# Weights of the gated layers and the output projection: loaded from the ScalarE queue instead of SyncE's, with the written-out order drawn up anew

## The chip, the cores and the metric

The kernel runs on one core of one Trainium2 chip. The metric is the device time of one execution in microseconds, as the median of several runs. The engines are called as in the profile: PE (TensorE, matmul; PEld is its weight load), DVE (VectorE), ACT (ScalarE), POOL (GpSimd) and SP (SyncE). A "q" behind a name (SPq, ACTq) means the sequencer of that engine, which issues DMAs.

## The reference, cut to what matters

Four layers are applied to one sequence x of 2048 rows and 512 columns, each with a layernorm ahead of it and a residual sum behind it: A, B, A, B. A is a linear attention whose features are softmaxes (32 heads of 16), B is a gated feed-forward layer of width 1376. Both A layers use the same weights, and so do both B layers.

```python
def _A_ref(x, wqkv, w_phi, wo):
    qkv = (x @ wqkv) ...                                   # split into q, k, v by head
    pq, pk = einsum(q, w_phi), einsum(k, w_phi)
    phi_q = concat([softmax(pq), softmax(-pq)]); phi_k = the same of pk
    kv = einsum("bhsf,bhsd->bhfd", phi_k, v);  z = sum_s phi_k
    o = einsum(phi_q, kv) / (einsum(phi_q, z) + 1e-6)
    return o @ wo                                          # output projection
def _B_ref(x, W_gate, W_up, W_down):
    gate = x @ W_gate;  up = x @ W_up
    gate = gate * (gate > 0)
    return (gate * up) @ W_down
x = x + _A_ref(layernorm(x), ...); x = x + _B_ref(layernorm(x), ...)   # twice
```

## The kernel before, in words

The sequence is cut into 16 row tiles of 128 rows. x stays in SBUF for the whole execution (`x_sb`), and is added to in place. The work goes by these names, which are the ones the recorded operations carry:

- `A0` and `A2` are the two attention layers, `B1` and `B3` the two gated layers, and `L0` to `L3` the layernorms ahead of them.
- In an attention layer, for every tile t: `k t` and `v t` (projections on PE, lines 725 and 766), `expk t` (ACT), `Zk t` and `rZk t` (sum and reciprocal on DVE), `phik t` (normalising, POOL or DVE), `kvacc t` (PE adds this tile to kv in two PSUM banks). Once all 16 tiles are in, `kvbd` and `kvf` on DVE take kv out of PSUM (`kv_fin`, line 792). Then the queries: `q t` or, for tiles 2 to 9 of A0, `q 2 c` and `q 6 c` for four tiles at once, `expq`, `num t` (PE), a division, `o t`, a transpose `otr t` and the output projection `wo t` (line 942), and `resid`.
- In a gated layer, for up to four tiles at once and for each of 11 slices fc of the width: `Wg` and `Wu` (PE, line 962; `gu` for the last, short slice), `relu` (ACT), on some slices `up` (ACT), `h` (DVE), and then `down t`, 11 matmuls that add all slices of tile t (line 1011), `resid`, and in the last layer `store`.
- Transposes of 128-row tiles (`L0 tr`, `A0 qtr`, `A0 otr`, `B1 htr`, `L1 tr`) are mostly done by DMA and issued by SP; tiles 0 to 3 of L0, and tiles 0 and 1 later on, are transposed on PE (`ytr`, `otr`, `tr`) and copied out by DVE or ACT.
- PE also gets 70 `dummy` matmuls on a tile of ones in the first 20 us, whose results are not used.

**What sets the order.** The kernel first records all operations, 3963 of them, with what each reads and writes. It doesn't order them itself: for each engine the string `ORDER` lists the numbers of its operations, in base 36, in the order in which they are issued, and `CHOICE` names an engine for those small operations that two engines can do (`op2`, line 433). `schedule` (line 229) goes through these lists with assumed durations and gives each operation a start. These assumed durations only decide how waits are numbered; [...]

**The weights that the change is about.** `late_weights` (line 605) records 18 loads from HBM: `wo0` to `wo3` (128 KB each, line 609), `Wg0` to `Wg3` and `Wu0` to `Wu3` (344 KB each, line 612), `Wd0` to `Wd4` (256 KB each, line 614) and `Wdl` (96 KB, line 615), some 4.5 MB together. Each takes as its read the transposed tile `("yT", 15)` of L0 (line 1061), so none can be issued before the transpose `L0 tr 15` has landed. They are first used by `A0 wo 0`, by `B1 gu 0 10` and the `B1 Wg` and `B1 Wu` behind it, and by `B1 down 0`, and stay in SBUF for the second pair of layers. The first loads of the kernel, x and the first attention weights, come earlier: x, `phi` and the transposed query weights `wqT` from SP, `wv` and `wk` from ACT (lines 542 to 555).

In the order before, the 18 loads stand in SP's list between transposes:

```
L0 tr 15, L0 tr 13, L0 tr 12, Wu2, L0 tr 14, Wd0, Wd4, wo1, Wdl, Wg1, A0 qtr 0 1, A0 qtr 0 0, Wd2, wo3,
A0 qtr 1 1, A0 qtr 1 0, Wg2, Wg0, wo0, Wg3, wo2, Wu0, Wd1, Wu1, Wu3, A0 otr 2, Wd3, A0 otr 3, B1 htr 0, ...
```

Of the kernel before, what the change touches and what calls it, by code (L numbers as in the profile page):

```python
# [14 lines left out]
        "29 26 6 25 27 28 2a 2b 4t 2c 39 49 3u 4y 4e 44 5i 5n 58 5s 4j 6j 6k 67 73 72 8l 6d 84 6a 4o 83 8k 91 9x 9y 7r 96 9z c4 c5 9b c6 9g d9 da db b4 f9 f8 "  # L15
        "fm fl ay ee ef b2 eg gz gy fz h0 hx hw fy ij g5 g4 ik gb ga gg gh ii hv mk mj n4 n3 mu mt lm lq lt ne nd nn no nt r8 o5 o4 rf of op oq jv kn p0 pa pb "
        "vg pl pw pv vk q6 qg qh qr s1 ko sd sc sn xw xt sx sy t8 lg tt tj ti zn u4 ue u3 zu up uo uz wd wo wp x9 wz xa m8 ru ym yn xk z7 11o z8 yx 10k 11s zi "
        "10l 11v 10v 142 w2 12t yb 149 146 134 13p 135 13f 109 159 14z 13q 15a 15u 12a 15v 15k 14o 16x 178 177 17i 1b7 16m 18l 1aw 1c9 1db 1ad 1by 1d0 1e6 1dv "
        "1ea 1f0 1fg 1ew 1em 1gj 1fw 1gk 1fc 1gi 1jm 1hk 1hl 1hj 1kb 1fs 1ib 1ic 1kr 1l7 1g8 1ia 1j2 1j3 1gx 1ll 1lk 1j1 1m9 1ma 1nv 1k6 1ob 1mz 1my 1lj 1or "
        "1l3 1kn 1p7 1nn 1m8 1mn 1no 1mx 1pl 1pk 1ly 1q9 1nm 1o7 1nc 1qa 1pj 1qz 1qy 1on 1rq 1rp 1q8 1s4 1p3 1qx 1s3 1py 1ro 1t5 1t6 1s5 1s6 1t8 1qn 1t7 1u7 "  # L20
        "1ua 1u8 1xr 1uw 1uv 1u9 1xx 1y3 1uy 1ym 1yn 1ux 1z1 1z2 1y9 1yl 1zh 1zg 1z0 1zv 1zw 1zf 24t 1zu 24u 255 24v 24w 256 258 230 257 25u 25t 25h 25i 25k "
        "25w 25v 25j 26q 271 27d 272 22j 27n 27c 27z 27o 27y 289 28a 28l 28k 28v 28w 297 29h 296 29i 29t 29s 2be 23c 23x 2bp 2bq 24i 2cc 2cb 2c1 26f 2c0 2dj "
        "2cn 2cm 2di 2dt 2b3 2e5 2du 2e4 2ef 2eg 2er 2eq 2ft 2fu 2hu 2i5 2i6 2ih 2ig 2j2 2ir 2j3 2a7 2is 2d7 2kg 2k6 2kh 2k5 2l2 2l3 2ks 2kr 2mh 2le 2mg 2ld "
        "2fi 2hb 2ju 2m5 2qa 2pz 2qb 2n8 2ql 2qw 2qx 2qm 2sa 2r7 2sl 2sb 2r8 2ny 2sw 2sx 2t7 2sm 2pg 2t8 2um 2tj 2ti 2ul 2g8 2rz 2mv 2ua 2vw 2x5 2ak 2v0 2xg "
        "2xr 2xh 2od 2y3 2xs 2y2 2vd 2yd 2yp 2ye 2yo 2z0 2zb 2yz 2zm 2za 2zl 2gl 2wo 2zw 2zx 308 2wb 307 30z 2oq 31c 30m 322 "),
    "dve": (
        "2z 30 33 3a 3b 3e 3l 3m 3v 3k 3w 3p 2m 53 3z 5d 5x 5z 5t 5v 5u 60 5y 5w 7i 7g 7f 7h 6l 64 6m ao 74 ap 75 an am 85 7t 86 8m a0 7x 8n 7v a3 a1 a4 c7 ca "
        "c8 cb dc df b0 fa dg fn dd fo fb eh ek el ei em h1 h2 fq h4 hy hz h5 i1 il im i0 in io j2 j1 j3 j4 ix jd iz je iy j0 k6 jj k7 ku ky l1 l2 jo l3 l4 jp "
        "l6 l7 lv lw ju kc ly lz nu kh rc rg ki rh og ld ri o6 le or p1 rk pc pm rl vn vo q7 m5 px vq qi m6 xp qs kp s2 vs so se r4 sz xy xz t9 rr tk tu y1 u5 "
        "uf uq zr 13s we lh v0 zw zx zy zz rs vc 13t vz x0 wq w0 y8 y9 xb yo xl 13v 106 107 17w yy 15x zj 15y m9 z9 17x 15z 10m 17y 1b9 1ba 19o 10w 12u 11y 181 "  # L30
        "19p 14c 120 121 136 118 14d 13g 16c 14e 16d 150 19r 1cb 127 11k 13r 15b w3 128 1cc 18b 18c 15w 15l 1cd 14l 14m 16y 16j 16k 17j 179 17v 18i 18j 1a3 1a4 "
        "1bo 1bp 19b 1cq 1cr 18z 1aa 1ab 1b8 1dl 1ax 1dm 19n 1bv 1cx 1bw 1cy 1ca 1e8 1ds 1dt 1e7 1eb 1dc 1ey 1fe 1f3 1fh 1d1 1en 1ex 1jk 1kp 1fu 1fx 1gl 1fj "
        "1ft 12b 1k9 1fd 1l8 1ks 1gy 1dw 1hm 1g9 1hn 1j4 1j5 1gm 1id 1ha 1go 1nt 1l5 1nw 1mb 1ie 1i1 1hp 1mc 1la 1o9 1is 1k7 1jj 1p5 1oc 1gn 1os 1op 1ko 1p8 "
        "1lm 1ln 1n0 1ig 1n1 1n2 1l4 1lo 1pm 1lz 1lp 1nd 1np 1mo 1j7 1nq 1pn 1po 1r0 1pp 1r1 1o8 1r3 1qb 1qc 1s7 1s8 1oo 1p4 1rr 1rs 1se 1sf 1pz 1qo 1t9 1tg "
        "1rf 1xp 1ta 1th 1qe 201 1xs 1sw 1xv 202 203 20f 1xu 1ty 1tl 204 20g 1y1 208 209 1yo 1um 1y7 1y6 1yp 1z3 1ya 1yq 1z4 1yc 1zi 1zj 1zl 1zx 1zy 200 1zz "
        "20a 21r 21q 21s 21p 20d 221 222 227 22u 22v 22c 23n 23o 22d 20m 22i 248 249 235 236 265 23b 20n 2et 26r 266 2gm 2eu 24f 23u 23v 273 2ev 27e 2gn 280 "
        "28b 27p 2at 24g 2au 28m 2go 2lg 298 2cx 29j 28x 29u 2cy 2j5 26c 2j6 26d 2n9 2na 2f8 2f9 2bf 23d 2a6 2lh 2br 2aj 2li 2ll 2b0 2h1 2cd 2c2 2h2 2d4 2ff "
        "2co 23y 2b1 2or 2os 2dk 2nc 2d5 2fg 2e6 2eh 2dv 2es 2tl 2fv 2jk 2jl 2g7 2ra 2ou 2b4 2hv 2rb 2i7 2ow 2lv 2tm 2lw 2gk 2it 2h8 2h9 2ii 2j4 2no 2m2 2k7 "
        "2np 2rf 2m3 2jr 2js 2l4 2ki 2kt 2p6 2p7 2lf 2mi 2mu 2rp 2nv 2nw 2rq 2n7 2m6 2u0 2u1 2qc 2q0 2hc 2jv 2op 2oc 2vm 2pd 2qn 2qy 2pe 2r9 2sc 2rw 2rx 2vn "
        "2t9 2sn 2sy 2tk 2un 2uz 2u7 2u8 2vt 2vu 2vc 2x6 2xt 2ub 2xi 2wa 2yf 2wn 2y4 2yq 2s0 2zn 2z1 2zy 2zc 309 30l 30y 31b 31o 320 "),  # L40
    "pool": (
        "2p 0 1 4 2t 5 2w 2x 31 2 2u 2n 2o 32 3c 34 3d 3n 3o 2y 3x 3y 3f 2s 2r 2q 2v 61 62 66 63 69 6c 3 7j 7l 7k 7m 7n 7o 6n 7p 7q 76 ar aq as au at 87 av aw "
        "ax 8o a2 a5 c9 cc dh fp fc de fd ff ej h3 fs en h6 l5 lu lx rj jw vp jx vr vt xx kq y0 zv y2 100 13u 13x 17z li 11w rv 160 11x 14a 14b ma 162 19q 1bb "
        "1be 11z 10a yc 19t 14f 1bc yd 1cg rw w4 1ce 10b 18m 14p 1ec 16n 1ed 1f1 1f2 1fi 1fy 1fz 1jn 1kc 1kd 1bz 18n 16o 1ke 14q 1jo 1kt 1jp 1c0 1ku 1l9 1ae "
        "1ho 12c 1nx 1p9 1dx 1pa 1if 1od 1md 1ny 1oe 1ot 1j6 1d2 1ou 1me 1n3 1af 1r2 1nr 1ns 1sg 1sj 1s9 1sc 1rt 1qd 1sa 1tb 1te 1tc 1xt 206 1sh 1ti 1tj 20h "
        "1y4 1y5 20k 1xy 1xz 1y0 1ru 1yr 1yb 1z6 1z5 1zk 20i 20b 20o 20r 20p 2ew 2gr 2gp 22k 22l 2ey 2j7 2j8 23e 26g 2ja 24j 2nb 24k 23z 2lj 2ot 2b5 2tn 2to "
        "2tq 2d8 26h 2ne 2rc 2rd 2d9 2hd 2fj 2fk 2nz 2o0 2jw 2vx 2ph 2m7 2s1 2pi 2uc 2vy "),
    "pe": (
        "7 8 9 a b c d e f g h i j k 4p 4q 4r 4s l m n o p q r s t u v w x y z 35 36 37 38 10 11 12 13 14 15 16 17 3g 3h 3i 3j 18 45 46 47 48 3q 3r 3s 3t 4z 50 "
        "51 52 59 5a 5b 5c 4u 4v 4w 4x 4a 4b 4c 4d 40 41 42 43 5e 5f 5g 5h 4f 4g 4h 4i 5j 5k 5l 5m 19 1a 1b 54 55 56 57 1c 1d 1e 5o 5p 5q 5r 1f 1g 6f 6g 6h 6i "  # L50
        "1h 6y 6z 70 71 1i 1j 1k 1l 1m 1n 1o 8g 8h 8i 8j 1p 1q 1r 1s 6p 1t 1u 7z 80 81 82 1v 1w 6o 1x 1y 1z 20 21 22 23 24 4k 4l 4m 4n 9l 9m 9n 9o 8x 8y 8z 90 "
        "9h 9i 9j 9k 9p 9q 9r 9s 9t 9u 9v 9w 6q 6r 6s 6t 77 78 79 7a 92 93 94 95 bo bp bq br bs bt bu bv 6u 6v 6w 6x 97 98 99 9a 88 89 8a 8b bw bx by bz c0 c1 "
        "c2 c3 ct cu cv cw 9c 9d 9e 9f cx cy cz d0 d1 d2 d3 d4 d5 d6 d7 d8 f4 f5 f6 f7 fh fi fj fk 7b 7c 7d 7e 8c 8d 8e 8f 8p 8q 8r 8s dy dz e0 e1 a6 a7 a8 a9 "
        "e6 e7 e8 e9 e2 e3 e4 e5 ea eb ec ed fu fv fw fx ae af ag ah cd ce cf cg cl cm cn co 8t 8u 8v 8w aa ab ac ad gm gn go gp gi gj gk gl ai aj ak al ch ci "
        "cj ck gq gr gs gt gu gv gw gx di dj dk dl g0 g1 g2 g3 hn ho hp hq dq dr ds dt ia ib ic id cp cq cr cs dm dn do dp hr hs ht hu g6 g7 g8 g9 du dv dw dx "
        "es et eu ev eo ep eq er gc gd ge gf ie if ig ih mb mc md me mf mg mh mi f0 f1 f2 f3 ew ex ey ez h7 h8 h9 ha hf hg hh hi i2 i3 i4 i5 ip iq ir is hb hc "
        "hd he hj hk hl hm i6 i7 i8 i9 it iu iv iw j5 j6 j7 j8 j9 ja jb jc mz n0 n1 n2 mv mw mx my k2 k3 k4 k5 jf jg jh ji jy jz k0 k1 ml mm mn mo mp mq mr ms "
        "kr ks kt kv kw kx kz l0 jk jl jm jn lj lk ll ln n5 n6 n7 n8 lo lp lr ls n9 na nb nc nf ng nh ni nj nk nl nm jq jr js jt k8 k9 ka kb r5 r6 r7 r9 np nq "
        "nr ns kd ke kf kg ob oc od oe o0 o1 o2 o3 nw nx ny nz ra rb rd re o7 o8 o9 oa ol om on oo oh oi oj ok l9 la lb lc os ot ou ov kj kk kl km p6 p7 p8 p9 "
        "p2 p3 p4 p5 vd ve vf vh ow ox oy oz m1 m2 m3 m4 pr ps pt pu pd pe pf pg pn po pp pq ph pi pj pk vi vj vl vm py pz q0 q1 q8 q9 qa qb q2 q3 q4 q5 qc qd "  # L60
        "qe qf qj qk ql qm xm xn xo xq rx ry rz s0 qn qo qp qq qt qu qv qw qx qy qz r0 r1 r2 r3 s8 s9 sa sb s4 s5 s6 s7 sf sg sh si xr xs xu xv sj sk sl sm sp "
# [295 lines left out]
ACT = mybir.ActivationFunctionType  # L357
AX = mybir.AxisListType
P = 128
# [17 lines left out]
CHOICE = {}  # L377
# [38 lines left out]
class Kernel:  # L416
# [96 lines left out]
    def setup(self):  # L513
        op, dma, r = self.op, self.dma, self.r
        k = self
# [698 lines left out]
```

The softmax here doesn't subtract the row's maximum and nothing guards it: scores larger than these inputs give would overflow.

## Time and profile before

| | |
|---|---|
| median of 8 runs | 379.36 us (378.92 to 379.82) |
| the profiled execution's own time | 379.82 us |
| its span, first to last instruction | 377.6 us |
| granted TensorE clock | 1.0 throughout |
| moved by DMA | 29.33 MB, of it 25.86 MB on SP's queue (q1) and 3.05 MB on ACT's (q10) |
| HBM read, written | 7.91 MB, 2.10 MB |

The page gives for each engine the time in which it was busy, then the span in 40 slices of 9.44 us with the busy share of each in tenths. A group of instructions carries its line, its tile and its mean duration. DMA issues carry the time that the sequencer took and the time from issue to landing. "A <- B" in an idle time means that A's wait ended with B. The profiled execution is one; its own time is 2.2 us more than its span and lies at the upper end of the runs.

### The profile page before, as it was taken

Reading aid. Unit: us, or ns where it says so; the run is one execution under the profiler, and the core shown is the slowest. Engines: PE = TensorE matmul, PEld = TensorE weight load, DVE = VectorE, ACT = ScalarE, POOL = GpSimd, SP = SyncE. Lnnn points to the kernel's source line nnn. Section 1 sums busy time; section 2 is a strip of 40 time slices with the busy share of each in tenths; the row PEclk is TensorE's granted clock in tenths of the full one; section 3 lists DMA queues with packets and bytes.
Section 4 is the critical chain, followed back from the end, with each engine's and each line's share of the span. In section 5 each row is a group of like instructions: output and inputs, shape, how many; then the busy total and the mean of one; then the engine's idle time right before and its main releaser. Section 6 shows DMA issues by size and latency. Waiting matters only on the chain.

```text
span 377.6 us, 6882 instructions
## 1 busy us (share of the span) xinstructions
PE 368.4 (98%) x2519; PEld 204.6 (54%) x2565; DVE 276.1 (73%) x607; ACT 227.0 (60%) x463; POOL 131.1 (35%) x234
## 2 busy tenths in 40 slices
PE   7999999999999999999999999999999999999997
PEld 5554555877744454454444446577664454445443
DVE  5999998989968666459799999898984654342323
ACT  3999878765744127874676568584635451653450
POOL 6799941132344001350463577023221201000020
PEclk9999999999999999999999999999999999999999
DMA  7632894313424444320300034435443442142012
GB/s 229 177 78 51 193 238 145 75 33 56 78 43 92 97 66 84 70 30 14 69 2 1 2 79 91 85 63 99 79 83 75 81 86 55 28 71 69 30 42 69
DMA packets 87856, 29.33 MB, mean 78 GB/s; under 512 B 79792, under 2 KB 86800, under 8 KB 87824
## 3 DMA queue, kind: packets, MB, share of 16 engines
q1 hardware_dynamic: 84368, 25.86, 33.7%
q10 hardware_dynamic: 3456, 3.05, 2.5%
q8 instruction: 20, 0.33, 0.4%
q14 instruction: 12, 0.10, 0.1%
HBM read 7.91 MB, written 2.10 MB: 27 GB/s over the span
## 4 chain that ended last, share of the span: by engine, by line
PE 84%; POOL 7%; DVE 3%; issue 2%; ACT 1%; DMA 1%; SPq 0%; POOLq 0%; DVEq 0%
PE ps L962 37%; PE ps L1011 20%; PE ps L725 7%; PE ps L942 7%; POOL expk L750 5%; PE ps L822 5%; PE ps L988 3%; PE ps L921 2%; DMA x_sb<-in_A_x_dram 1%; PE ps L787 1%; PE ps L886 1%; DVE Zk L744 1%; POOL rstd L648 1%; PE ps L868 1%; DVE expk L755 0%
## 5 line engine op out<-in xcount | busy, mean ns | idle before, releaser
L962 PE MATMUL ps<-yT,Wgu 128*128 128x512 bf16 (+2 forms) x870 | 150.8, 320 | 0.6
L962 PEld LDWEIGHTS ps<-yT,Wgu 128*128 128x128 bf16 x880 | 78.5, 98 | 58.8 <-ACT expk L970 1.0
L964 ACT ACTIVATE gate_sb<-ps 128x512 bf16<-128x512 f32 (+2 forms) x110 | 50.7, 480 | 55.3 <-PE ps L962 41.2
L1011 PE MATMUL ps<-Wd,hT 128*128 128x512 bf16 (+4 forms) x354 | 79.3, 373 | 0.5
L1011 PEld LDWEIGHTS ps<-Wd,hT 128*128 128x128 bf16 (+1 forms) x363 | 34.7, 98 | 39.5 <-DVE hT L972 0.7
L972 DVE TENSOR_TENSOR hT<-gate_sb,expk 128x512 bf16<-128x512 bf16 (+2 forms) x70 | 23.9, 360 | 30.4 <-ACT expk L970 21.4
L970 ACT ACTIVATE expk<-ps 128x512 bf16<-128x512 f32 (+2 forms) x70 | 32.0, 475 | 22.2 <-PE ps L962 19.5
L710 ACT ACTIVATE sq<-x_sb,nmr 128x512 bf16<-128x512 bf16 x48 | 34.6, 721 | 10.3 <-DVE x_sb L687 6.6
L744 DVE TENSOR_REDUCE Zk<-expk 128x64 f32<-128x1024 bf16 x32 | 38.1, 1203 | 0.9 <-ACT expk L737 0.7
L714 POOL TENSOR_TENSOR rstd<-rv,mone 128x1 f32<-128x1 f32 x32 | 18.7, 589 | 50.2 <-DVE rv L712 50.0
L1013 DVE SCALAR_TENSOR_TENSOR x_sb<-ps,rstd,x_sb 128x512 bf16<-128x512 f32 (+2 forms) x33 | 23.9, 728 | 15.9 <-PE ps L1011 13.2
L942 PE MATMUL ps<-wo_p,oT 128*128 128x512 bf16 x118 | 30.9, 379 | 0.6 <-DVE oT L413 0.3
L975 DVE TENSOR_TENSOR hT<-gate_sb,ps 128x512 bf16<-128x512 bf16 (+2 forms) x40 | 21.7, 544 | 12.6 <-ACT gate_sb L964 6.4
L855 POOL TENSOR_TENSOR expq<-expq,rho 128x256 bf16<-128x256 bf16 x36 | 22.2, 624 | 24.4 <-DVE rho L852 23.6
L847 DVE TENSOR_REDUCE Zq<-expq 128x64 f32<-128x1024 bf16 x24 | 28.8, 1204 | 0.8 <-POOL rho L852 0.5
L687 DVE SCALAR_TENSOR_TENSOR x_sb<-ps,x_sb 128x512 bf16<-128x512 f32 x32 | 21.9, 687 | 8.6 <-PE ps L942 7.8
L750 POOL TENSOR_TENSOR expk<-expk,rZk 128x1024 bf16<-128x1024 bf16 x13 | 25.9, 2005 | 0.6 <-DVE rZk L746 0.6
L755 POOL TENSOR_TENSOR expk<-expk,rZk 128x512 bf16<-128x512 bf16 x17 | 19.1, 1134 | 11.8 <-DVE rZk L746 11.5
L822 PE MATMUL ps<-Wqp,yT 128*128 128x512 bf16 x91 | 22.7, 379 | 0.3
L725 PE MATMUL ps<-Wkp,yT 128*128 128x512 bf16 x84 | 22.0, 379 | 0.2
L725 PE MATMUL ps<-wv_p,yT 128*128 128x512 bf16 x85 | 21.9, 379 | 0.2
L712 POOL TENSOR_SCALAR rv<-rv 128x1 f32<-128x1 f32 x22 | 4.4, 205 | 45.1 <-ACT sq L710 45.1
(126 smaller groups left out, 515.4 us busy)
## 6 DMA issues: line engine op xcount, KB each, us to landing
out_dram<-x_sb ACTq DMA_DIRECT2D x15, 128.0 KB, 1.7
x_sb<-in_A_x_dram SPq DMA_DIRECT2D x3, 512.0 KB, 5.2
Wgu<-in_B_W_up_dram SPq DMA_DIRECT2D x4, 344.0 KB, 6.1
Wgu<-in_B_W_gate_dram SPq DMA_DIRECT2D x4, 344.0 KB, 4.2
Wd<-in_B_W_down_dram SPq DMA_DIRECT2D x5, 256.0 KB, 3.6
yT<-ytile SPq DMA_TRANSPOSE x56, 2.5
qT<-expq SPq DMA_TRANSPOSE x40, 2.5
hT<-in_A_wqkv_dram ACTq DMA_DIRECT2D x4, 128.0 KB, 4.3
```

Source lines behind the costliest of these rows:

```text
L710: op("act", lambda e: e.activation(k.sq[:], k.x_sb[:, t, :], ACT.Square, scale=-float(D), bias=k.nmr[:, t, :], accum_out=k.rv1[:, t, :]), ...
L725: op("pe", (lambda ic, bank, W: lambda e: e.matmul(k.pb[bank][:], k.yT[:, ic, t * 128:(t + 1) * 128], W[:, ic, :], start=(ic == 0), stop=( ...
L744: op("dve", lambda e: e.tensor_reduce(k.Zk[:, zb, :], k.expk[:, t, :, :, :].rearrange("p g s (h f) -> p (g s h) f", f=16), AX.X, ALU.add), ...
L750: op("pool", lambda e: e.tensor_tensor(kv, kv, k.rZk[:, rb, :].unsqueeze(2).to_broadcast([P, 64, 16]), ALU.mult), [r("expk", t, 0), r("exp ...
L822: op("pe", (lambda ic, bank, tt: lambda e: e.matmul(k.pb[bank][:], k.yT[:, ic, tt * 128:(tt + 1) * 128], k.Wqp[:, ic, :], start=(ic == 0), ...
L847: op("dve", lambda e: e.tensor_reduce(k.Zq[:, b, :], k.expq[:, t, :, :, :].rearrange("p g s (h f) -> p (g s h) f", f=16), AX.X, ALU.add), ...
L942: op("pe", (lambda c, bank: lambda e: e.matmul(k.pb[bank][:], k.oT[:, ob, c, :], k.wo_p[:, c, :], start=(c == 0), stop=(c == NC - 1)))(c, ...
L962: op("pe", (lambda bank, W, ic, fc, Mf: lambda e: e.matmul(k.pb[bank][0:Mf, 0:n], W[:, ic, fc * 128:fc * 128 + Mf], k.yT[:, ic, c0:c0 + n] ...
L964: op("act", (lambda Mf, gb, gs: lambda e: e.activation(k.gate_sb[0:Mf, gs, 0:n], k.pb[gb][0:Mf, 0:n], ACT.Relu))(Mf, gb, gs), [self.RP[gb] ...
L970: op("act", (lambda Mf, ub, up: lambda e: e.activation(up[0:Mf, 0:n], k.pb[ub][0:Mf, 0:n], ACT.Copy))(Mf, ub, up), [self.RP[ub]], ru, 170 ...
L972: op("dve", (lambda Mf, up, gs, u: lambda e: e.tensor_tensor(k.hT[0:Mf, u, 0:n], k.gate_sb[0:Mf, gs, 0:n], up[0:Mf, 0:n], ALU.mult))(Mf, u ...
L1011: op("pe", (lambda fc, Kf, u, c0, bank, m0, m1: lambda e: e.matmul(k.pb[bank][:, m0:m1], k.hT[0:Kf, u, c0:c0 + 128], k.Wd[0:Kf, fc, m0:m1] ...
```

## The change

Four things change; the recorded operations, what they compute and what they depend on stay the same 3963.

1. The 18 loads of `late_weights` are recorded for ACT's queue, no longer for SP's.
2. `ORDER` is another order for all five engines, from the first instruction to the last. The loads now stand among ACT's operations (below). SP's list holds transposes and first loads only.
3. `CHOICE` sends 97 small operations from POOL to DVE or back (49 to DVE, 48 to POOL), five copies from DVE to ACT (`L0 ytrcopy 1`, `A0 otr 0 copy`, `A0 numcp 5 2`, `6 0`, `7 1`) and five from ACT to DVE (`A0 numcp 3 1`, `6 2`, `8 1`, `9 0`, `9 2`).
4. An assumed duration (the first activation, with its table load: 1450 became 250) and the way in which `L0 apply` names its second possible engine. No `L0 apply` changes its engine by it.

```diff
 late_weights:
-   ... dma("sp", lambda e: e.dma_start(k.wo_p[:, c, :], self.A_wo[...]), [rd], [r("wo", c)], 131072, f"dma wo{c}")
+   ... dma("act", lambda e: e.dma_start(k.wo_p[:, c, :], self.A_wo[...]), [rd], [r("wo", c)], 131072, f"dma wo{c}")
-   ... dma("sp", lambda e: e.dma_start(W[:, c, :], src[...]), [rd], [r(nm, c)], 128 * F * 2, f"dma {nm}{c}")
+   ... dma("act", lambda e: e.dma_start(W[:, c, :], src[...]), [rd], [r(nm, c)], 128 * F * 2, f"dma {nm}{c}")
-   ... dma("sp", lambda e: e.dma_start(k.Wd[:, 2 * j:2 * j + 2, :], ...), [rd], [r("Wd", j)], 262144, f"dma Wd{j}")
+   ... dma("act", lambda e: e.dma_start(k.Wd[:, 2 * j:2 * j + 2, :], ...), [rd], [r("Wd", j)], 262144, f"dma Wd{j}")
-   ... dma("sp", lambda e: e.dma_start(k.Wd[0:96, 10, :], ...), [rd], [r("Wd", 5)], 96 * 1024, "dma Wdl")
+   ... dma("act", lambda e: e.dma_start(k.Wd[0:96, 10, :], ...), [rd], [r("Wd", 5)], 96 * 1024, "dma Wdl")
 setup:
-   op("act", ... ACT.Exp), [r("ones")], [r("sq"), r("tbl")], 1450, "table")
+   op("act", ... ACT.Exp), [r("ones")], [r("sq"), r("tbl")], 250, "table")
 ln:
-   self.op2("act" if on_act else "dve", apply, dep, dst, {"dve": 407, "act": 825}, f"{tag} apply {t}", 250.0)
+   how = CHOICE.get(f"{tag} apply {t}", "act" if on_act else "dve")
+   other = "act" if how == "dve" else "pool" if t < 9 and how == "act" else "dve" if how == "act" else "act"
+   dd = {"dve": 407, "act": 825, "pool": 2090}
+   self.op2(how, apply, dep, dst, {e: dd[e] for e in (how, other)}, f"{tag} apply {t}", 250.0)
 ORDER, CHOICE: all strings new
```

ACT's new list around the loads, in names:

```
... A0 expk 10 1, A0 expk 10 0, wo0, Wu2, L0 apply 14, A0 vcopy 10, A0 expk 12 0, A0 expk 12 1, Wg1, Wu1,
A0 vcopy 12, A0 expq 2 0 0, Wu0, A0 expk 14 1, wo3, A0 expk 14 0, A0 expq 2 0 1, A0 expq 2 1 0, A0 expk 15 0,
A0 expq 2 1 1, A0 expk 15 1, A0 expq 2 2 0, Wd2, A0 expq 2 2 1, A0 expq 2 3 0, A0 expq 2 3 1, Wg2, A0 vcopy 14,
wo2, A0 vcopy 15, A0 expq 6 0 0, Wg3, A0 expq 6 0 1, wo1, Wu3, Wd4, A0 otr 0 copy, Wg0, A0 expq 10 1, ...
B1 relu 0 10, A0 numcp 4 0, B1 up 0 0, B1 relu 0 0, Wdl, A0 numcp 4 2, B1 relu 0 1, B1 up 0 2, L1 var 0, Wd0,
B1 relu 0 2, L1 tr 1 copy, Wd3, B1 relu 0 3, A0 numcp 5 0, B1 relu 0 5, B1 relu 0 4, Wd1, B1 up 0 4, ...
```

SP's list begins `x0, x3, x1, x2, phi, x4, x8, wqT, x12` (before: `x0, x1, x3, x2, phi, x4, x8, x12, wqT`), ACT's `wk0, table, wv2, wv0, wv1, wv3, wk2, wk1, wk3` (before: `wk0, wv1, table, wv0, wv2, wv3, wk1, wk2, ...`).

## The prediction

> **What bounds the kernel now.** I read the page first (busy shares and slices), then PE's waits, then the busy time by stretches, then the issues of SP and the two other queues around the loads.
>
> ```profile
> PE 368.4 (98%) x2519; PEld 204.6 (54%) x2565; DVE 276.1 (73%) x607; ACT 227.0 (60%) x463; POOL 131.1 (35%) x234
> ...
> PE   7999999999999999999999999999999999999997
> ...
> DVE  5999998989968666459799999898984654342323
> ACT  3999878765744127874676568584635451653450
> ```
>
> PE is busy 368.4 of 377.6 us. At most 9.2 us of idle time, and the dummies, are to be had at all. The waits of PE that the profile names are fewer still:
>
> ```profile
> PE ps L539 <- POOL ones L527: 1.6, 1, 1.6
> PE ps L678 <- DVE ytile L670: 0.9, 1, 0.9
> PE ps L886 <- DVE expk L413: 0.5, 1, 0.5
> PE ps L942 <- DVE oT L413: 0.3, 1, 0.3
> ```
>
> They are 4.2 us in all with four smaller ones; 1.6 is the start of the program. No named wait is on a late weight. The busy time by stretch says where another engine stands behind PE (columns: stretch, length, then PE, PEld, DVE, ACT, POOL busy):
>
> ```profile
> 16.00:53.00 37.00, 36.73 (x296) 19.53 (x299) 36.51 (x52) 35.36 (x54) 33.90 (x37) 1.00 0.58 114
> ...
> 54.00:66.00 12.00, 11.01 (x81) 6.05 (x83) 10.16 (x26) 8.10 (x11) 1.50 (x3) 1.00 0.55 183
> 66.00:75.00 9.00, 8.90 (x119) 7.43 (x120) 8.56 (x27) 7.03 (x23) 1.22 (x4) 1.00 0.33 72
> 75.00:225.00 150.00, 149.15 (x878) 78.23 (x894) 118.84 (x263) 88.37 (x194) 53.81 (x101) 1.00 0.28 51
> ```
>
> From 16 to 53 us four engines are full at once: PE, DVE (36.51 of 37), ACT (35.36), POOL. DVE's chain there sets when kv is complete. After 75 us PE has nothing to gain: 0.85 idle in 150. So a change can help only in the first 66 us, and can hurt anywhere. Around the loads SP looks like this:
>
> ```profile
> 43.24 0.43 SPq L612 DMA_DIRECT2D Wgu<-in_B_W_gate_dram  x1
> 43.71 2.50 SPq L858 DMA_TRANSPOSE qT<-expq  x2
> 46.26 0.58 SPq L614 DMA_DIRECT2D Wd<-in_B_W_down_dram  x1
> ```
>
> One load costs SP 0.43 to 0.58 us, a transpose about 1.25. SP works through the loads from 38.5 to 55.2, and one more at 65.5. And ACT, where they go:
>
> ```profile
> 45.15 1.09 ACT L737 ACTIVATE expk<-ps 128x512 bf16<-128x512 f32 x2 [0.49 <-PE ps L787]
> ...
> 48.51 2.14 ACT L871 ACTIVATE expq<-ps 128x512 bf16<-128x512 f32 x4
> ```
>
> From 45.15 to 51.6 ACT runs back to back; its idle times in 37 to 53 are 0.53, 0.49 and 0.33.
>
> [...] The trace agrees that position in the row matters: most transposes land 2.5 us after issue, the two that transpose qT at 43.71, behind five loads, land 6.1 and 5.3 us after theirs. [...] The trace of before shows what this means for an ACT that issues a DMA, in a store of the last layer:
>
> ```profile
> 290.00 1.09 ACT L964 ACTIVATE gate_sb<-ps 128x512 bf16<-128x512 f32 x2 [2.20 <-PE ps L962]
> 290.78 0.35 ACTq L1023 DMA_DIRECT2D out_dram<-x_sb  x1
> 290.97 1.09 ACT L970 ACTIVATE expk<-ps 128x512 bf16<-128x512 f32 x2
> ```
>
> The next activation starts at 290.97, 0.48 after the one ahead of it (290.49), the pitch it also has with no DMA between. SP was issuing a transpose then, and the store's issue was no longer (0.35).
>
> **The change, part by part.** The sum is made against the profiled execution (span 377.6, own time 379.82).
>
> *SP is freed.* 18 issues, 0.43 to 0.68 each, 9.0 us. Who waited for them? The transposes behind them: `L0 tr 14`, `A0 qtr 0` and `1`. Tile 14 landed at 42.6 and its k runs at 44.1. The q transposes landed at 49.9 to 52.4 and `num 0` runs at 53.66, after kvbd on DVE. All covered by the DVE chain, at least 1.2 us to spare. Gain 0; if that cover were gone it would be 3 us.
>
> *ACT gets 18 issues.* Thirteen stand between 38 and 54 us, each behind activations with a pitch of 0.48 (512 columns) or 0.92 (1024). By the store an issue hides behind one activation. Where two or three stand together (wo0 and Wu2, Wg1 and Wu1, wo1 with Wu3 and Wd4) issue exceeds cover: 1.03 against 0.92, 1.0 against 0.92, 1.5 against 0.92. That is 0.1, 0.1 and 0.6; the last falls before ACT's 2.2 us idle at 54 to 56. ACT's idle 0.53, 0.49, 0.33 swallows the others. Bounds: 0, and 6 x 0.48 = 2.9 us ahead of `expk 15 1` if nothing hides. I take 0. The wait of wo0 on tile 15's transpose is new on ACT, with `L0 apply 14` behind it; that transpose landed at 36.7, and ACT reaches the load at about 38.2. Cost 0, with 1.5 us to spare.
>
> *The loads land where they are used.* wo0 to wo3 before 60 us and Wg, Wu before 65.7: last issued are wo1, Wu3 and Wg0 at 54 to 57.5, landing times of 3.3 to 6.8 are seen, so 61 to 64: fits. Wdl, Wd0, Wd3 and Wd1 are now issued among the relus of `B1`, from 68 on; the latest is Wd1, reckoned under the rivals. I take 0.
>
> *The start.* x1 is now the third SP load, not the second. Second and third landed at 3.99 and 6.11 before, the fourth at 6.87. DVE's lines there:
>
> ```profile
> 5.47 0.35 DVE L666 TENSOR_SCALAR ytile<-x_sb,mv 128x512 bf16<-128x512 bf16 x1
> 6.89 0.69 DVE L623 BATCH_NORM_STATS2 stats<-x_sb 128x6 f32<-128x512 bf16 x1 [1.07 <-DMA x_sb<-in_A_x_dram]
> ...
> 8.30 0.41 DVE L413 COPY yT<-ps 128x512 bf16<-128x512 bf16 x1
> ```
>
> DVE idled 1.07 for x2. Now it idles from 4.6 to about 6.1 for x1, 1.5, and then x2 is there. Against that, the copy at 8.30 (0.41) goes to ACT, which idles then. On DVE: 1.5 - 1.07 - 0.41 = 0.0. On PE `v 1` stands behind the transpose of tile 2, whose `apply 2` moves behind BD (0.69) and comes 0.5 to 0.9 later; `comp wk 0` is now ahead of it; I reckon `v 1` at 10.4 for 10.18. ACT, full from there to the first expk, passes this on: +0.2. Bounds: if x1 lands 0.5 earlier, because ACT's second load now stands behind the table activation and its wait for the ones (about 1.6 instead of 1.24), -0.3; if it doesn't and tile 3 slips too, +0.6.
>
> *Everything else* is the same operations in another order. From 16 to 53 DVE has the same set of work. In 54 to 66 DVE loses the copy of otr 0 (0.36) and gets ab 2, zm 3 and numcp 3 1 (about 1.1) for zd 2 and zd 3 (0.37), while L1 apply 0 moves behind tsc 2: by my count 64.4, and PE asks for it at 64.67. 0. After 75 us I take 0; PE's waits there have no room to gain 0.8.
>
> Sum: 0 + 0 + 0 + 0.2 + 0 = +0.2. Span 377.8, own time 380.0; the median stands 0.46 below that execution, so 379.56, that is **379.6**. A measurement of this kernel can tell about 0.2%, 0.76 us, from no change, so this is no change.
>
> **The rivals.**
> *ACT's issues are not hidden* (slower). 2.9 us ahead of `expk 15 1`; ACT's idle takes 1.0, and from its end (48.68) to Zk 15 (49.48) there are 0.8. DVE's chain, and with it kv, would be 1.1 late, the later issues add up to 0.7: 381.4. It decides from 0.30 us per issue (1.8 over six). Against it: the store above, but that ACT had just idled.
> *Wd1 comes late* (slower). It stands behind relu 0 5 and relu 0 4: before, relu 0 3 and 0 4 ran at 70.71, numcp takes 0.55, two relus about 0.5, so issue at 71.8. These loads took 2.9 (alone) to 3.6 (median) to land: 74.7 to 75.4. `down 0` starts at 74.98 and wants it at its third matmul, 75.4. From 3.6 us on each further tenth is one of PE; at 4.5, +0.9: 380.5.
> *A new stall in the dense part* (slower). The order is new for 300 us in which PE waited for nothing. Some transposes need 4.1 to 4.3 us, not 2.5; an order that has only 0.6 to spare loses 1.1 once: 380.7.
> *Faster.* The copy off DVE counts (0.4), x lands earlier (0.3), and of the 0.5 that PE idles around the second kv, 225 to 250, most goes: -0.9 to -1.1 against my sum, 378.5. For it: DVE's chain of the first layer has next to no gaps. Against it: ACT must follow.
> *The loads hide anyway*, so that the change of queue does nothing and only the order counts, is what my sum says.
>
> **How the numbers follow.** No change 0.37 (its own range 378.7 to 380.3); faster 0.27; ACT not hidden 0.13, Wd1 late 0.12, new stall 0.11, together slower 0.36. The range leaves out the far end of faster (below 378.2, 0.08) and of the slow cases (above 381.4, 0.10): 378.2 to 381.4.
>
> **What would show it.** Right: ACT's pitch of 0.48 and 0.92 stays with loads between; transposes of q land in 2.5 to 4 us; kvbd at 53.0 to 53.4; `down 0` without a wait; PE's idle after 75 us as before. Wrong: idle of ACT with nothing released by another engine at the loads; a wait of line 1011 on a DMA; stats of tile 1 later than 6.3; a PE wait above 0.5 us behind 75 us.

## The result, and the profile after

The kernel after takes **381.35 us** in the median of 12 runs (380.08 to 382.07), the kernel before beside it 379.36 in 32. The ratio is 1.0043 with a 95% interval of 1.0034 to 1.0053: slower by 0.4%, small and certain. The forecast was no change at 379.6; the time lies inside the range (378.2 to 381.4), by 0.05 at its upper edge.

The runs don't lie evenly. Five are between 380.08 and 380.49, seven between 381.24 and 382.07, and none in between; the kernel before has nothing of the kind (378.76 to 380.5; of 94 later runs of it, beside the experiments, one is above that, 381.01). So there are two things to find: what costs every run about 0.9 us, and what costs half of them 1.3 more. The profiled execution of the kernel after took 380.14 and has a span of 378.4 (before: 377.6), so it is one of the lower group. Behind the layernorm's code its lines stand three later than in the kernel before (725 is 728, 766 is 769, 886 is 889, 1011 is 1014).

The page of the kernel after, busy time and slices:

```profile
PE 367.1 (97%) x2520; PEld 203.1 (54%) x2565; DVE 277.6 (73%) x608; ACT 227.1 (60%) x463; POOL 123.5 (33%) x233
...
PE   6999899999999999999999999999999999999997
```

PE has an 8 in its fifth slice (37.8 to 47.3 us). Every slice behind it is as full as before. PE's waits say what the 8 is:

```profile
PE ps L539 <- POOL ones L527: 1.6, 1, 1.6
PE ps L769 <- DMA yT<-ytile: 1.4, 1, 1.4
PE ps L681 <- DVE ytile L669: 1.3, 1, 1.3
```

The second line is new: a k projection waits 1.4 us for a transpose by DMA. The third is the start, where PE now idles for x1 (before, 0.9 for another tile). The busy time by stretches shows where the time is lost and where not (length, then PE, PEld, DVE, ACT, POOL, as in the prediction):

```profile
16.00:53.00 37.00, 35.20 (x252) 18.06 (x256) 35.61 (x51) 34.08 (x52) 33.77 (x37) 1.00 0.57 113
...
75.00:225.00 150.00, 149.10 (x893) 78.52 (x907) 121.00 (x269) 87.04 (x193) 47.34 (x95) 1.00 0.28 51
```

In 16 to 53 us PE, DVE and ACT all lost busy time (36.73 to 35.20, 36.51 to 35.61, 35.36 to 34.08): a gap that stops the three of them. After 75 us PE is as busy as before (149.10 for 149.15). The gap itself, in ACT's part of the timeline (start, length, engine, line, operation):

```profile
36.03 0.34 ACTq L609 DMA_DIRECT2D wo_p<-in_A_wo_dram  x1
36.17 0.85 ACT L662 ACTIVATE ytile<-x_sb,nmr,rstd 128x512 bf16<-128x512 bf16 x1
36.40 0.58 ACTq L612 DMA_DIRECT2D Wgu<-in_B_W_up_dram  x1
36.88 1.98 ACT L772 ACTIVATE expk<-ps 128x1024 bf16<-128x1024 f32 x2
...
42.57 1.02 ACT L772 ACTIVATE expk<-ps 128x1024 bf16<-128x1024 f32 x1 [2.10 <-PE ps L769]
```

`wo0` and `Wu2` stand in ACT's list behind both `expk` of tile 10. Those run at 36.88 to 38.86, but the loads went out at 36.03 and 36.40: 0.85 and 0.48 us before the first of the two activations that stand ahead of them had begun. While they went out ACT still ran `L0 apply 12` (line 662), whose result is what `L0 tr 12` transposes. So the loads overtook the very transpose that the k of tile 12 waits for. `L0 tr 12` follows at 37.05 on SP. The DMA issues of that moment (KB, then time from issue to landing), first of the kernel before, then of the kernel after:

```profile
yT<-ytile SPq DMA_TRANSPOSE x1, 2.4
```

```profile
Wgu<-in_B_W_up_dram ACTq DMA_DIRECT2D x1, 344.0 KB, 4.5
yT<-ytile SPq DMA_TRANSPOSE x1, 4.4
```

The transpose is the same and from the same queue, issued 0.2 earlier than before (37.05 for 37.27). It landed 1.8 later, at 41.45 for 39.69.

### The profile page after: what moved, and what is told of

Its sections match the earlier page's. It is cut to its first block, busy times and chain, and to the rows that moved or that the text cites. A ratio compares the mean times of both kernels' runs of the same rounds, so it can differ in the third digit from the quotient of the medians.

```text
span 378.4 us, 6894 instructions
## 1 busy us (share of the span) xinstructions
PE 367.1 (97%) x2520; PEld 203.1 (54%) x2565; DVE 277.6 (73%) x608; ACT 227.1 (60%) x463; POOL 123.5 (33%) x233
## 4 chain that ended last, share of the span: by engine, by line
PE 91%; DVE 2%; DMA 2%; ACT 2%; issue 1%; SPq 0%; ACTq 0%
PE ps L965 37%; PE ps L1014 20%; PE ps L728 10%; PE ps L945 7%; PE ps L825 5%; PE ps L769 3%; PE ps L991 3%; PE ps L790 2%; PE ps L871 2%; PE ps L924 2%; DMA yT<-ytile 1%; PE ps L889 1%; DMA x_sb<-in_A_x_dram 1%; ACT expq L830 1%; DVE stats L623 1%
## 5 line engine op out<-in xcount | busy, mean ns | idle before, releaser
L1014 PE MATMUL ps<-Wd,hT 128*128 128x512 bf16 (+3 forms) x356 | 79.6, 372 | 0.4
L975 DVE TENSOR_TENSOR hT<-gate_sb,expk 128x512 bf16<-128x512 bf16 (+2 forms) x70 | 22.9, 343 | 26.0 <-ACT gate_sb L967 17.3
L747 DVE TENSOR_REDUCE Zk<-expk 128x64 f32<-128x1024 bf16 x32 | 38.2, 1205 | 4.3 <-ACT expk L740 3.0
L715 POOL TENSOR_SCALAR rv<-rv 128x1 f32<-128x1 f32 x33 | 6.2, 193 | 79.4 <-ACT sq L713 79.2
L717 POOL TENSOR_TENSOR rstd<-rv,mone 128x1 f32<-128x1 f32 x32 | 17.8, 562 | 20.3 <-DVE rv L715 19.5
L855 POOL TENSOR_TENSOR rho<-rZq,Zq 128x32 f32<-128x32 f32 x17 | 4.8, 286 | 57.8 <-DVE rZq L854 41.4
L758 POOL TENSOR_TENSOR expk<-expk,rZk 128x512 bf16<-128x512 bf16 x18 | 20.2, 1130 | 8.9 <-DVE rZk L749 8.3
```

The costliest lines, as they stand in the source:

```text
L747: op("dve", lambda e: e.tensor_reduce(k.Zk[:, zb, :], k.expk[:, t, :, :, :].rearrange("p g s (h f) -> p (g s h) f", f=16), AX.X, ALU.add), ...
L1014: op("pe", (lambda fc, Kf, u, c0, bank, m0, m1: lambda e: e.matmul(k.pb[bank][:, m0:m1], k.hT[0:Kf, u, c0:c0 + 128], k.Wd[0:Kf, fc, m0:m1] ...
```

## The experiments

All are compared with the kernel before on the same chip. Their lines stand 15 or 16 later than in the kernel they are made from, since `ORDER` is written on more lines. "Lower" and "upper group" are the two groups of times above. The first theory: the loads that go out early share the DMA engines with `L0 tr 12`, and this wait is the loss. Where they are set against the kernel after, that is by its 12 runs above; beside the experiments it was executed only twice more (E0 below).

### The two loads later, the same queue (E1)

```diff
 ACT: ... expk 10 1, expk 10 0,
-  wo0, Wu2,
   L0 apply 14, vcopy 10, expk 12 0,
+  wo0, Wu2,
   expk 12 1, Wg1, Wu1, ...
```

`expk 12 0` waits for the k of tile 12. In the kernel after, the next load behind it in the list, `Wg1`, left at 42.58, 0.01 us after `expk 12 0` had begun (42.57, after 2.10 us of waiting for PE). So the two loads, too, should leave only when `L0 tr 12` has landed.

> The kernel after, with one edit: wo0 and Wu2 stand in ACT's list behind A0 expk 12 0 instead of behind A0 expk 10 0. Theory (the two loads go out ahead of L0 tr 12 and share the DMA engines with it): L0 tr 12 lands within 3 us of its issue instead of 4.4, the wait of L769 on its DMA (1.4 us) is gone, and the median is 379.4 to 380.0, 1.3 to 1.9 below the kernel after. Rival 1 (the new order is slower by itself, whatever the loads do): 381 to 381.5, as after. Rival 2 (ACT's time for issuing them is what costs): 381 to 381.5, as after, since ACT issues as many. Rival 3 (tile 12 is late by chance or by instruction fetches): the wait stays at about 1.4.

Measured: **379.46** (ratio 1.001, 0.9999 to 1.0022). `L0 tr 12` landed 2.42 us after issue; PE's list of waits names no DMA any more; its longest are the start (1.7 for x1, 1.6) and then one of 0.5. The loads went out at 41.73 and 42.10, the first at the moment in which `expk 12 0` began. Moving two of 18 issues takes back 1.9 us of the median, so neither the queue nor the issuing as such costs that. Two groups are still there: nine runs from 378.87 to 379.71, five from 380.24 to 380.9. Their medians lie 1.1 and 0.9 below those of the two groups of the kernel after; the rest of the 1.9 is that fewer runs are in the upper one.

### The new order, the loads on SP (E2)

```diff
 late_weights: dma("act", ...) -> dma("sp", ...), all four lines
 SP: ... L0 tr 15, L0 tr 13, L0 tr 12,
+  Wu2,
   L0 tr 14,
+  Wd0, Wd4, wo1, Wdl, Wg1,
   A0 qtr 0 0, A0 qtr 0 1, ...          (the rest as in the kernel before)
```

> The order, the choices and the start of the kernel after, but all 18 loads on SP's queue again, between the transposes where the kernel before has them (Wu2 behind L0 tr 12). Theory: no load is in flight when L0 tr 12 is, the wait of L769 on a DMA is gone, 379.0 to 379.8. Rival 1 (the new order): 381 to 381.5. Rival 2 (ACT's issuing): 379.0 to 379.8 too, with ACT's idle ahead of expk 12 0 shorter; this run doesn't tell it from the theory. Rival 3: the wait of 1.4 stays.

Measured: **379.42** (1.0003, 0.9992 to 1.0014), 12 of 14 runs from 379.12 to 379.61. The new order by itself costs nothing that can be measured.

### The old order, the loads on ACT (E3)

```diff
 late_weights: dma("sp", ...) -> dma("act", ...), all four lines
 SP: the 18 loads taken out
 ACT: ... expk 10 1,
+  wo0, Wu2,
   L0 apply 14, ...                     (the other 16 at neighbours like those in the kernel after)
```

> The order, the choices and the start of the kernel before, but the 18 loads on ACT's queue, wo0 and Wu2 behind A0 expk 10 1 as in the kernel after and the others behind neighbours like those they have there. Theory: L0 tr 12 lands over 4 us after its issue, the k of tile 12 waits 1 to 2 us for it, 380.5 to 381.3. Rival 1 (the new order): 379.2 to 379.6, as before. Rival 2 (ACT's issuing): about 381, with idle time of ACT at the loads that no other engine ends.

Measured: **380.71** in six runs (380.04 to 381.66; 1.0041, 1.0026 to 1.0055), by the ratio as large a loss as that of the kernel after, with the old order and the old start. The trace is of the slowest of the six. Its waits:

```profile
PE ps L782 <- DMA yT<-ytile: 1.6, 1, 1.6
PE ps L1027 <- DMA Wd<-in_B_W_down_dram: 1.0, 1, 1.0
```

The first is tile 12's again, 4.7 us from issue to landing. Here `Wu2` was issued at 37.45, *after* `L0 tr 12` at 37.11: the issue of a transpose takes SP 1.19 us, that of the load 0.45, and the load in the other queue still landed first (41.45, the transpose at 41.79). `wo0`, issued at 37.08, was in flight beside both, so this run alone doesn't say which load it was; E9 below does for the kernel after. The second line is a wait for the last weight of `down 0`; it comes back below.

### Wu2 ahead of the transpose, in SP's own queue (E5)

```diff
 SP (kernel before): ... L0 tr 13,
+  Wu2,
   L0 tr 12,
-  Wu2,
   L0 tr 14, ...
```

> The kernel before, with one edit: Wu2 stands on SP just ahead of L0 tr 12 instead of just behind it. ACT issues none of the loads. Theory: what counts is that the load is issued ahead of the transpose, in whichever queue; tr 12 lands 4 us or more after its issue, its k waits 1 to 2 us, 380.5 to 381.0. If only the going out on a second queue matters, or if ACT's issuing is the cause (rival 2): 379.4 to 379.8, with at most 0.4 from the later issue of tr 12.

Measured: **380.15** (1.0028, 1.0019 to 1.0036), between the two expectations. `L0 tr 12` was issued at 38.01, 0.74 later than before, and needed 3.1 us; the wait is a third of the other:

```profile
PE ps L781 <- DMA yT<-ytile: 0.5, 1, 0.5
```

So here an early `Wu2` harms in either queue. From issue to landing the transpose needed 3.12 us behind `Wu2` in SP's queue, 4.40 and 4.68 beside it in ACT's, alone 2.4. But in SP's queue the issue of the load also held the transpose back, so that it landed 1.4 us later than before, for 1.8 in the kernel after. ACT as the issuer isn't needed for a loss.

### Only Wu2 later (E9)

```diff
 ACT: ... expk 10 1, expk 10 0, wo0,
-  Wu2,
   L0 apply 14, vcopy 10, expk 12 0,
+  Wu2,
   expk 12 1, Wg1, Wu1, ...
```

> The kernel after, with one edit: only Wu2 (344 KB) moves behind A0 expk 12 0; wo0 (128 KB) stays where it is, issued before L0 tr 12. Theory: what delays tr 12 is the bulk that is still in flight when it is issued; wo0 alone has landed by 38.5 and takes at most 0.5 us from tr 12: its wait is 0.3 us or less, and the median lies 1.1 to 1.5 below the kernel after, 379.4 to 380.3. If one load of any size ahead of it does the same harm: the wait stays at 1.2 to 1.4, 381 to 381.5.

Measured: **378.99** (0.9993, 0.9985 to 1.0001), better than expected. `wo0` went out at 36.07, as in the kernel after, and had landed at 38.49; `L0 tr 12`, issued at 37.10, took 2.40. The busy time in the same microsecond, in the kernel after and then in this one (PE is the first figure behind the length, the last two are the DMA share and GB/s):

```profile
40.00:41.00 1.00, 0.07 (x1) 0.00 (x0) 1.00 (x2) 0.47 (x1) 1.00 (x2) 1.00 0.94 207
```

```profile
40.00:41.00 1.00, 1.00 (x6) 0.44 (x5) 1.00 (x2) 0.52 (x1) 1.00 (x2) 1.00 0.16 33
```

With `Wu2` in flight the DMA engines move 207 GB/s in it, 94% busy, and PE stands still from 40.07 to 41.5; without it they are 16% busy and PE is full. It is the one bulk load of 344 KB, not the first issue of any size. Where the transpose loses its time shows two microseconds earlier, again in the kernel after and then in this one:

```profile
38.00:39.00 1.00, 1.00 (x14) 0.53 (x11) 0.97 (x3) 1.00 (x2) 1.00 (x1) 1.00 0.86 73
```

```profile
38.00:39.00 1.00, 1.00 (x15) 0.52 (x12) 0.97 (x3) 1.00 (x2) 1.00 (x1) 1.00 0.79 156
```

In the kernel after the DMA engines are busy, but move little. From 38.25 to 39.25 only 24 packets start, all of `Wu2`: they fill 80% of the engines' time at 66 GB/s, the longest takes 1.06 us, and SP's queue starts no packet from 38.22 to 39.39. In E9 546 packets of SP's queue start in the same stretch. So the transpose first stands still while the first packets of the load are under way, and only then do packets of both queues run: from 39.39 to 41.5 SP's transposes take 61.5% of the engines' time, the rest of the load 31.3%. Why its first packets take so long isn't shown.

Twelve of the 13 runs are in one group (378.89 to 379.48), 1.3 below the lower group of the kernel after, which is the wait and no more; one is above it (380.58). Why the upper group is so thin here isn't shown: this edit touches neither the start nor the late loads.

### What the upper group is: three kernels about the start (E6, E7, E8)

E2's trace is of one of its two upper runs (380.84), and it shows PE at half its rate early on: three v matmuls take 1.48 us, where the lower trace of the kernel after has 0.81 (in both the record of a fourth one is missing). E2's trace, then the lower one of the kernel after:

```profile
7.66 0.58 PE L696 MATMUL ps<-ident,ytile 128*128 128x128 bf16 x4 [1.30 <-DVE ytile L684]
...
9.21 1.48 PE L743 MATMUL ps<-wv_p,yT 128*128 128x512 bf16 x3 [0.22 <-DVE hT L575]
```

```profile
7.97 0.81 PE L728 MATMUL ps<-wv_p,yT 128*128 128x512 bf16 x3
```

That gave a second theory: in the upper group PE, idle for the late x1, hasn't come to its full rate when the v of tile 0 arrives. Three edits of the kernel after go at it.

```diff
E6, SP:   x0,
+  x1,
   x3,
-  x1,
   x2, phi, ...
E7:       E6 and E1 together
E8, PE:   ... ytr 0, dummy 27 to 34,
+  dummy 35 to 48,
   ytr 1,
-  dummy 35 to 41,
   v 0, ..., wtr wk 3,
-  dummy 42 to 48,
   comp wk 1, ...
```

> The kernel after, with one edit: x1 is the second load on SP's queue, as in the kernel before, not the third. Theory of the start: x1 lands at about 4.0 us, DVE and PE don't idle for it, PE keeps its rate, and the upper group of times is gone: all or nearly all runs within 379.7 to 380.4, median 380.0 to 380.2, since the wait for L0 tr 12 stays. If the two groups have another cause, they stay, with about half of the runs in each, and the median is near 381.

> The kernel after, with both edits: wo0 and Wu2 behind A0 expk 12 0 on ACT, and x1 second on SP. Theory: the two losses are separate and both gone: 378.8 to 379.3, one group of times, equal to the kernel before or up to 0.5 faster. If the start is neutral, as with the two loads moved alone: 379.4 to 379.5 with two groups of times.

> The kernel after, with one edit: 14 dummy matmuls (35 to 48), which stand behind the transposes of tile 1 and behind wtr wk 3, stand ahead of the transposes of tile 1, in the time in which PE idles for x1. The loads and their order are those of the kernel after. Theory of the start: PE idles 0.5 us or less for x1, comes to its full rate ahead of v of tile 0 in all or nearly all runs, and the upper group of times is gone: median 380.1 to 380.5. If the late x1 itself makes the upper group, and not PE's rate, both groups stay and the median is near 381.

Measured: E6 **380.16** (1.0022, 1.0014 to 1.0031; 379.82 to 380.51), E7 **379.02** (0.9997, 0.9988 to 1.0005; 378.8 to 379.66 and one of 380.07), E8 **380.34** (1.0027, 1.0017 to 1.0038; 379.96 to 380.72). The times came as the theory said: no upper group in E6 and E8. E6 and E7 have the same start and differ in the two loads alone: the wait for `L0 tr 12` costs **1.14 us**.

### The same with the sign turned, and two more traces of the kernel after (E10, E0)

```diff
E10, PE:  ... ytr 0,
-  dummy 27 to 34,
   ytr 1, dummy 27 to 33 (were 35 to 41), v 0, ..., wtr wk 3,
+  dummy 34 to 41,
   dummy 42 to 48, comp wk 1, ...
E0:       the kernel after, unchanged
```

> The kernel after, with one edit, the opposite of the dummies put earlier: the eight dummy matmuls (27 to 34) ahead of the transposes of tile 1 are gone from there, and eight more stand behind wtr wk 3. PE is idle from about 5.3 us until x1 is there. Theory of the start: PE comes to its full rate ahead of v of tile 0 in fewer runs than in the kernel after; over three quarters of the runs are in the upper group, 381.2 to 382.1, and the median is 381.5 or more; the three v matmuls of tile 0 take 1.5 us in the trace if it is of that group. If the dummies don't matter: the two groups as in the kernel after, about half and half, or fewer.

> The kernel after, unchanged, for another trace of it. The times of the kernel after fall in two groups, 380.1 to 380.5 and 381.2 to 382.1; its trace is of the lower one. Theory of the start: in the upper group PE has not come to its full rate when it idles for x1, from about 6 us, and the three v matmuls of tile 0 that follow take 1.5 us instead of 0.8. If this trace is of the upper group, it shows that, and the first SP transpose of tile 5 is issued 1 us or more later than 16.88; if it is of the lower group, the v matmuls take 0.8. In both, k of tile 12 waits 1.2 us or more for L0 tr 12.

> The kernel after, unchanged, once more for a trace of its upper group, which neither trace of it so far shows. If it is: v of tile 0 takes 1.5 us, as in the trace of the new order with the loads on SP. If not: a time within 380.1 to 380.8.

Measured: E10 **382.03** (1.0072, 1.0055 to 1.0089; 381.09 to 383.35, all six above every run of the lower group). The time is what the theory asked for, but the trace isn't: from 7.17 us PE did four transposes in 0.38 us (E2's trace: 0.58), and the four v matmuls took 1.03. The first further trace of the kernel after, of 380.74, lies between the groups and shows nothing new but x1 landing at 6.32 where the first had 5.62. The second, of **381.73**, is of the upper group:

```profile
7.73 1.03 PE L728 MATMUL ps<-wv_p,yT 128*128 128x512 bf16 x4
```

Four v matmuls in 1.03: full rate. Its list of waits has the reason elsewhere:

```profile
PE ps L769 <- DMA yT<-ytile: 1.4, 1, 1.4
PE ps L1014 <- DMA Wd<-in_B_W_down_dram: 1.4, 1, 1.4
```

`down 0` waits 1.4 us for `Wd1`. In this trace, as in E10's (1.3) and E3's (1.0), `Wd1` needs 5.3 to 5.6 us; in the lower trace of the kernel after, issued at the same time (72.44 and 72.49), 3.2. The lower one, then the upper one:

```profile
Wd<-in_B_W_down_dram ACTq DMA_DIRECT2D x1, 256.0 KB, 3.2
```

```profile
Wd<-in_B_W_down_dram ACTq DMA_DIRECT2D x1, 256.0 KB, 5.3
```

So the second theory falls for the kernel after; v at half rate is what E2's trace has, and none of the three traces of the kernel after has it. In the three traces with the wait, packets of `Wd1` are still unsent when those of a transpose start (`A0 otr 4` in two, `L1 tr 2` in E3's). The queues' packets from 75.5 to 78 us in the upper trace of the kernel after (queue, packets, MB, share of 16 engines):

```profile
q1 hardware_dynamic: 653, 0.16, 70.4%
q8 instruction: 1, 0.02, 2.3%
q10 hardware_dynamic: 9, 0.01, 1.2%
```

Nine packets of `Wd1` (q10) stand beside the transposes (q1) and one instruction fetch of 16 KB (q8, 0.92 us). In the lower trace the load had landed, at 75.61, before that. The fetch may matter more than the transposes: it runs from 75.80 to 76.72, and no packet of `Wd1` starts from 75.76 to 76.71; in E10's trace the same holds from 76.03 to 76.95. In the lower trace the fetch began at 74.54, and the last packets of `Wd1` ended at 75.27. A few tenths seem to decide, and the difference is over two microseconds of landing time. The two traces of the kernel after are alike up to there: `L0 tr 12` and `Wd1` are issued within 0.05 us of each other in both, so that in this pair the wait of `down 0` is 1.4 of the 1.6 us between the spans (380.0 for 378.4). All this is read from traces, not from an edit: a kernel after in which only the late Wd loads are moved wasn't run. Nor is it settled why E6 and E8, which don't touch these loads, were never in the upper group and E10 always. E6 and E8 ran on one chip, E10 on another; whether the share of upper runs depends on the chip wasn't tested (E1, on the chip of E6, has five of 14).

### The old order, the loads on ACT at better places (E11)

```diff
 E3, ACT: ... expk 10 1,
-  wo0, Wu2,
   L0 apply 14, vcopy 10, expk 12 1, expk 12 0, Wg1, Wu1,
+  wo0, Wu2,
   expq 2 0 1, ..., expq 10 1, expq 10 0,
+  Wdl, Wd0, Wd3, Wd1,
   ..., B1 relu 0 0,
-  Wdl, (and Wd0, Wd3, Wd1 further on)
```

> The order, the choices and the start of the kernel before, with the 18 loads on ACT's queue: the first four behind A0 expk 12 0, and Wdl, Wd0, Wd3 and Wd1 behind A0 expq 10 0, so that down 0 doesn't wait for Wd1 as it did (1.0 us) with the old order and the loads on ACT at the new places. Theory: the queue itself costs nothing; no wait of PE on a transpose or a weight, 379.0 to 379.6, as before, in one group of times. Rival 2 (ACT's issuing costs): 380 or more.

Measured: **378.93** in 21 runs (378.54 to 379.99), ratio 0.9989 with an interval of 0.9982 to 0.9995: a little faster than the kernel before, and than the kernel after by 2.4 us. `Wd1` landed at 62.7, 12 us ahead of its use. The transposes of the first q tile took 8.2 and 9.1 us in this kernel, and PE waited for none of them; its waits behind the start are 0.5, 0.3 and 0.2. E3 and E11 differ in the places of six loads alone (`wo0`, `Wu2` and the four late ones), and 1.8 us lie between their medians: with the old order, where these six stand is the whole loss. How it divides between the two places isn't told by this pair. So the change of queue in itself is harmless, and up to 0.4 us good. What that gain comes from was not taken apart.

## Why the prediction was right or wrong

**The sum.** The number is inside its range by luck: its upper edge was left open for other losses (ACT's issues not hidden, 381.4), and what came is two terms that the sum had at nothing. The wait for `L0 tr 12` costs 1.1 us in every run (E6 against E7). The upper group costs 1.3 more in seven of twelve; that this is `Wd1` is read from one trace of it. The rest was 0 to -0.3 (E7 stands 0.26 below the kernel before, within the interval). 1.14 + 1.3 - 0.3 is 2.1; the medians are 2.0 apart. The mean of the runs, with which the ratio is made, has the second term at half: 1.6.

**The step that failed** is the one on ACT's 18 issues: "that transpose landed at 36.7, and ACT reaches the load at about 38.2. Cost 0, with 1.5 us to spare." ACT's sequencer issued the load at 36.03, 2.2 us earlier. The prediction had the store of the last layer before it, whose issue of 0.35 us left the pitch of 0.48 as it was. It used this to hide the issue time, rightly, and not to ask when a load that runs beside activations leaves. In the kernel after the two loads went out with two activations ahead of them not yet begun (36.03 and 36.40 for 36.88). Behind an activation that had to wait for PE this was not so: in E1 `expk 12 0` waited 0.51 us and began at 41.73, and `wo0` left at 41.73. So the order of ACT's list doesn't tell by itself whether a load leaves ahead of the activations before it.

**The step that was left out** follows from it. "SP is freed" asked which transposes had stood behind a load before, and found them covered: right. The sign "transposes of q land in 2.5 to 4 us" failed (3.9 to 5.5 in the lower trace, 3.4 to 9.1 in all those with the loads on ACT), but no list of waits names one. It didn't ask which transposes get a load beside them now. `L0 tr 12` had no load ahead of it before (`Wu2` stood behind it in SP's queue) and its k is next on PE. The sum counted that SP's queue is rid of the loads, not that they would then run beside its transposes. Both show: from issue to landing `L0 tr 12` needed 2.4 us alone, 3.1 behind the load in one queue, 4.2 to 4.7 beside it in two. For 1.2 us of that (38.22 to 39.39) only the load's packets started.

**The loads land where they are used**: right for wo, Wg and Wu (the last, Wg0, at 60.69). For `Wd1` the rival *Wd1 comes late* had the mechanism and the place, `down 0`, with a chance of 0.12 and 0.9 us at a landing time of 4.5. Where it came, landing took 5.3 and the wait 1.4. Both of the signs for it are in that trace: a wait of line 1011 (now 1014) on a DMA, and a PE wait above 0.5 us behind 75 us. A transfer with 0.7 us of slack (in the lower trace it landed at 75.61; `down 0` began at 75.89, its first record is missing, and its third matmul would want it at 76.3) isn't "0" where others run beside it. In the ten traces that issue it between 71 and 73 us it took 2.8 to 3.2 or 5.3 to 5.6 to land, and nothing in between. The prediction's 75.4 for the third matmul in the kernel before is 0.2 late for the same reason: the weights of the first were loaded at 74.71, so the matmul shown at 74.98 is the second.

**The start**: +0.2 forecast; E7, with x1 second, stands 0.13 below the nine lower runs of E1, the same kernel with x1 third. x1 landed at 5.62 and 6.32 in two traces, 5.65 in the third; the transpose of tile 5 was issued up to 0.1 earlier than before in two of them and 0.6 later in one. The sign "stats of tile 1 later than 6.3" showed in the slower of them only.

**Right**: ACT's pitch stays 0.48 with a load in between (`Wd2` went out at 49.99, `Wg2` at 50.86, `wo2` at 51.27):

```profile
49.99 0.60 ACT L874 ACTIVATE expq<-ps 128x512 bf16<-128x512 f32 x1 [0.43 <-PE ps L871]
49.99 0.41 ACTq L614 DMA_DIRECT2D Wd<-in_B_W_down_dram  x1
50.48 0.59 ACT L874 ACTIVATE expq<-ps 128x512 bf16<-128x512 f32 x1
```

The next two activations follow at 50.96 and 51.44. An issue took 0.33 to 0.58, the activation ran on, so the rival *ACT's issues are not hidden* is out. *A new stall in the dense part* is out in the lower trace: after 75 us PE lost nothing in it. kvbd came at 54.0 for the 53.0 to 53.4 forecast; with only `Wu2` moved it comes at 52.9 (E9). *Faster* was there to be had (E11; E9's interval still holds no change), but not with these places.

## What to carry to other kernels

A DMA in an engine's list can leave before the work ahead of it has begun: here 0.85 and 0.48 us before, past two activations. What held it back here was a place behind an activation that waited for PE (E1: `wo0` left at 41.73, as `expk 12 0` began). When a bulk load changes queue, look for the small transfers in the *other* queues that will now be in flight with it, and what waits for each: `Wu2` landed at 40.9 and PE first reads its tile at 66.8, while the k of tile 12 waited 1.4 us for the transpose beside it. Transfers that land just in time are worth trying earlier, as long as the room is there: in E11 `Wd1` landed 12 us ahead of its use, and PE didn't wait for it. A time that falls in two groups can be a hint that one of them sits on such an edge; here that is read from one trace of the upper group, and E2's upper run had another reason.

## What the runs showed of the hardware that was not expected

- A transpose landed late beside a load issued *after* it in another queue: the transpose at 37.11, `Wu2` at 37.45, landing 4.7 us after issue for 2.4 (E3, with `wo0` of 37.08 beside both). The transpose's own issue took 1.19 us, a load's mostly 0.33 to 0.6.
- The DMA engines were full once without moving much: 24 packets of `Wu2` took 80% of their time at 66 GB/s from 38.25 to 39.25 (the kernel after), and no packet of the other queue started.
- PE's rate early in the kernel differs from run to run. The same three matmuls took 1.48 us in one trace and 0.81 in others, with like idle times ahead of them (1.30, and 1.26 and 1.80). The full rate shows from different times on. In E6 four transposes took 0.39 us at 4.83, and in E2 0.63 at 4.86. In the upper trace eight dummies took 1.06 at 5.31, where the lower one has 0.61 at 5.27, and four transposes 0.38 at 7.12. In E2 seven dummies still took 0.95 at 8.04, where the lower trace has 0.55 at 7.36. What sets the rate isn't shown: the column of the granted clock is 1.0 in all stretches.
